# Weights converted by a leaky rectifier, a rounding copy and an integer addition; softmax sums in PSUM, pooled scale in the queries

## The chip, the cores and the metric

One core of a Trainium2 chip runs the whole program. The metric is the device time of one execution in microseconds (us), less is better. The core has five engines that run side by side, each strictly in the order of its own list of instructions: PE (TensorE, the matrix multiplier, whose weight loads are listed as PEld), DVE (VectorE), ACT (ScalarE), POOL (GpSimd) and SP (SyncE, which here only issues DMA transfers). They wait for one another by semaphores. SBUF is the working memory, PSUM the memory that matmuls write; DVE and ACT reach both, POOL reaches SBUF.

## The reference

Attention over 8 batches, 8 heads, 576 positions and 64 values a head, in two parts that are added: one over a band of neighbours (distance below 4), one over sequences pooled by 4. Then a feed-forward layer over all 4608 tokens.

```python
q_d, k_d, v_d = (a.reshape(B, H, Sd, 4, D).mean(axis=3) for a in (q, k, v))
out_up = np.repeat(sm_attn(q_d, k_d, v_d), 4, axis=2)      # softmax(q k^T / 8) v, pooled
scores = np.where(np.abs(i - j) < 4, q @ k.T / 8, -1e9)     # local band
out_local = softmax(scores) @ v
x = (out_up + out_local) as (4608, 512)
h = x @ w_in                                                # 512 -> 2048
g = np.where(h >= 1, h, np.where(h <= -1, 0, (h + 1) ** 2 / 4))
out = g @ w_out                                             # 2048 -> 512
```

The weights arrive as 64-bit floating point numbers, and the kernel's host part passes them on as pairs of 32-bit words; the device makes 32-bit numbers of them.

## The kernel before

*Attention.* The 64 heads are worked in 32 pairs; pair `n` covers two heads of one batch, so four pairs fill one batch of 576 tokens. `attention(n, ...)` is a generator, and each `yield` is a place where other work can be put between. For one pair: DVE pools queries and keys by sums over four (`qd` L150, `kd` L157), ACT puts `qd` into a block-diagonal tile `q_bd` (L153). PE makes the band's scores in windows of 64 (`sl_ps` L166) and the pooled scores (`sp_ps` L176). For the band, DVE adds the mask (L184) and finds the maxima (L191), POOL subtracts them (L192), ACT takes the exponential (L195), DVE sums the rows (L211), adds 1e-9 (L212), inverts (L213) and scales (L214). For the pooled part, DVE finds three maxima (L202) and multiplies them by minus the scale (L203), ACT takes three exponentials of 96x144 straight out of `sp_ps`, each with its row sum as a second output (L205), DVE adds 1e-9 and inverts (L218, L219), ACT scales (L221). PE transposes both (`tl_ps` L233, `tp_ps` L242), ACT copies them out, PE multiplies them with the values (`pl_ps` L261, `pp_ps` L273), ACT and DVE add the two (`xd` L282, `x` L284), and ACT and POOL split the sum into a high and a low part (`xh` L293, `xl` L294). `sp_ps` has a bank of 512 columns of PSUM, of which 432 are used.

*Weights.* `load_weights(f)` fetches block `f` of 16 of both weight matrices (`raw_i`, `raw_o`, 512 KB each). `convert_weights` makes a 32-bit number of each 64-bit one: the upper word, read as a 32-bit float and scaled by ACT (L319), is brought to the right sign and bits by DVE (L320, L321); DVE masks the exponent (L323), scales the lower word with it (L324) and adds it (L327). ACT rounds the sum to the type that PE multiplies (L329) and POOL keeps the rest (L330). Each of the 32 conversions takes one buffer named `m` from a ring of four tiles of 512 columns (`t512`), which the feed-forward's `u`, `osb` and `first` also use.

*Feed-forward.* `mm1(c, f)` multiplies 384 tokens (chunk `c` of 12) with block `f` of `w_in` into `h_ps` (12 matmuls, L408); ACT, DVE and POOL make `gh` and `gl` of it (L419 to L425). `mm2(c, f)` multiplies these with `w_out` into three accumulators `o_ps` (9 matmuls, L446). Chunk 0 needs the first four pairs, chunk 2 the pairs up to the eighth; the first half of all blocks is done for chunks 0 and 2 before the second half is needed.

*Order.* Two lists of steps (`BEFORE_STEPS`, `FIRST_STEPS`) say in which order pieces of attention (`a0` to `a11`), loads (`w`), conversions (`c`), `mm1` (`s`) and `mm2` (`m`) are written for the beginning; then a loop puts one pair between every few feed-forward steps. The framework's scheduler takes this as priority and decides each engine's own order from it, so that a changed set of instructions moves others too. SP issues all transfers from one list: a load into a buffer that is still in use holds those behind it.

Of the kernel before, what the change touches and what calls it, by code (L numbers as in the profile page):

```python
# [99 lines left out]
def attention_then_ffn(ctx: ExitStack, tc, qT, kT, vw, vp, band, w_in, w_out, out):  # L100
    nc = tc.nc
# [37 lines left out]
    def small(n, tag):  # L139
        return apool.tile([P, n], F32, name=tag, tag=tag, bufs=2)  # L140

    def attention(n, pool_1, pool_2):

        b, p = pairs[n]
        q, k = qk[p] if b == 0 else (loaded["q"], loaded["k"])
        M = 2 * QB


        qd = apool.tile([P, SD], F32, name="qd", tag="qd", bufs=1)
        nc.vector.tensor_reduce(qd, q.rearrange("p (s f) -> p s f", f=FACTOR), axis=AX.X, op=ALU.add)  # L150
# [32 lines left out]
        slf = sl.rearrange("p g r c -> p (g r) c")  # L183
# [4 lines left out]
            op=ALU.add,  # L188
# [14 lines left out]
        nc.vector.tensor_scalar_mul(mx[:M], mx[:M], -scale)  # L203
        for i in range(NQB):
            nc.scalar.activation(  # L205
                sp[:M, i], sp_v[:, i], AF.Exp,
                bias=mx[:M, i : i + 1], scale=scale, accum_out=sm[:M, i : i + 1],
            )
# [3 lines left out]
        nc.vector.tensor_scalar_add(ll, ll, 1e-9)  # L212
        nc.vector.reciprocal(ll, ll)  # L213
        nc.vector.tensor_tensor(  # L214
            slf, slf, ll.unsqueeze(2).broadcast_to([P, NB, WIN]), op=ALU.mult
        )
        yield
        nc.vector.tensor_scalar_add(sm[:M], sm[:M], 1e-9)  # L218
# [51 lines left out]
        for kb in range(NKB):  # L270
            for h in range(2):
                hs = slice(h * D, (h + 1) * D)
# [17 lines left out]
            op=ALU.add,  # L290
# [17 lines left out]
    def temp(name):  # L308
        return mpool.tile([P, 512], F32, name=name, tag="t512", bufs=4)

    def convert_weights(name, f):

        t = raw.pop((name, f))
        tf = t.bitcast(F32)
        m = temp("m")
        mi = m.bitcast(I32)


        nc.scalar.activation(m, tf[:, :, 1], AF.Copy, scale=2.0**-112)  # L319
        nc.vector.scalar_tensor_tensor(m, m, -(2.0**32), m, op0=ALU.mult, op1=ALU.max)  # L320
        nc.vector.tensor_scalar(mi, mi, 3, None, op0=ALU.logical_shift_left)  # L321

        nc.vector.tensor_scalar(t[:, :, 1], mi, 0xFF800000 - (1 << 32), None, op0=ALU.bitwise_and)  # L323
        nc.vector.scalar_tensor_tensor(  # L324
            tf[:, :, 0], t.bitcast(U32)[:, :, 0], 2.0**-52, tf[:, :, 1], op0=ALU.mult, op1=ALU.mult
        )
        nc.vector.tensor_tensor(m, m, tf[:, :, 0], op=ALU.add)  # L327
        w = wpool.tile([P, 2, 512], F32R, name=f"w_{name}{f}", tag=f"w{name}{f}")
        nc.scalar.copy(w[:, 0], m)  # L329
        nc.gpsimd.tensor_tensor(w[:, 1], m, w[:, 0], op=ALU.subtract)  # L330
        weights[name, f] = w
# [197 lines left out]
```

## Time and profile before

| | |
|---|---|
| median of 3 runs | 1023.12 us (1021.39 to 1025.07) |
| profiled execution | 1023.42 us |
| its span, first to last instruction | 1021.6 us |
| PE busy | 968.0 us, 95% |
| DVE busy | 444.4 us, 44% |
| ACT busy | 518.7 us, 51% |
| POOL busy | 410.7 us, 40% |

The profile is of one execution. A view by stretches gives each engine's busy time between two moments, a view by groups puts together the instructions of one line, operation and shape: `x17 | 14.2, 834 | 0.3` are 17 instructions, 14.2 us in all, 834 ns each, and 0.3 us for which the engine sat idle before them, with what ended that idle time. A row of waits gives the engine and line that waited, what it waited for, and the us in total, the times, and the longest. The row PEclk gives PE's granted clock in 40 equal slices, in tenths of full speed.

### The profile page before, as it was taken

How to read it: one execution, taken by the hardware profiler on the slowest of the kernel's cores; microseconds unless marked ns; L12 is line 12 of the kernel's file. 1: busy time of each engine (PE TensorE's matmuls, PEld its weight loads, DVE VectorE, ACT ScalarE, POOL GpSimd, SP SyncE). 2: the span in 40 equal slices, each digit the busy share in tenths (PEclk: the TensorE clock that was granted, in tenths of full speed). 3: DMA queues.
4: the chain of work that ended last, by engine and by line, in shares of the span. 5: the costliest groups of instructions: out<-in, count | busy, mean ns of one | idle time of the engine just before them, and what ended most of it. 6: DMA issues, size and time to landing. Idle time of an engine off the chain costs nothing.

```text
span 1021.6 us, 18401 instructions
## 1 busy us (share of the span) xinstructions
PE 968.0 (95%) x7412; PEld 851.1 (83%) x7412; DVE 444.4 (44%) x774; ACT 518.7 (51%) x1189; POOL 410.7 (40%) x359
## 2 busy tenths in 40 slices
PE   5577898999999999999999999999999999999998
PEld 4465687889988888999888888899888888899997
DVE  7999979754344533112433443111443344111111
ACT  5556564545455655434655565433655546433433
POOL 3566655453345444322435444322443544222221
PEclk8579899999999999999999999999999999999999
DMA  7666410000133311100212311100311320000000
GB/s 267 220 232 209 151 56 1 31 24 32 34 117 102 113 48 50 55 1 24 80 48 69 102 54 49 56 1 1 102 49 48 98 72 21 31 1 1 32 1 31
DMA packets 28261, 69.37 MB, mean 68 GB/s; under 512 B 3344, under 2 KB 3344, under 8 KB 28176
## 3 DMA queue, kind: packets, MB, share of 16 engines
q1 hardware_dynamic: 28176, 68.20, 20.7%
q8 instruction: 58, 0.95, 0.4%
q14 instruction: 27, 0.22, 0.1%
HBM read 57.18 MB, written 11.01 MB: 67 GB/s over the span
## 4 chain that ended last, share of the span: by engine, by line
PE 79%; DVE 12%; issue 3%; ACT 3%; POOL 1%; DMA 1%; SPq 0%; DVEq 0%; ACTq 0%; POOLq 0%
PE h_ps L408 35%; PE o_ps L446 34%; PE sp_ps L176 2%; PE sl_ps L166 2%; DVE m L320 2%; PE pl_ps L261 2%; PE pp_ps L273 2%; PE tl_ps L233 2%; PE tp_ps L242 1%; DVE m L327 1%; DVE raw_o L324 1%; DVE raw_i L324 1%; DVE u L421 1%; DVE raw_o L323 1%; DVE m L321 1%
## 5 line engine op out<-in xcount | busy, mean ns | idle before, releaser
L408 PE MATMUL h_ps<-xh,w_i 128*128 128x384 f32 x1536 | 403.4, 344 | 7.5 <-DVE u L421 5.2
L425 POOL TENSOR_TENSOR gl<-u,gh 128x384 fp32r<-128x384 f32 x192 | 208.2, 1085 | 480.3 <-ACT gh L424 374.4
L446 PE MATMUL o_ps<-w_o,gh 128*128 128x512 f32 x1152 | 358.4, 392 | 1.6 <-ACT gh L424 1.6
L408 PEld LDWEIGHTS h_ps<-xh,w_i 128*128 128x128 f32 x1536 | 277.7, 190 | 24.2 <-DVE u L421 7.1
L421 DVE SCALAR_TENSOR_TENSOR u<-h_ps,u 128x384 f32<-128x384 f32 x192 | 106.5, 555 | 435.8 <-ACT u L420 409.5
L408 PE MATMUL h_ps<-xl,w_i 128*128 128x384 f32 x768 | 261.8, 341 | 2.7 <-POOL xl L294 2.7
L446 PEld LDWEIGHTS o_ps<-w_o,gh 128*128 128x128 f32 x1152 | 213.2, 188 | 35.7 <-ACT gh L424 2.5
L446 PE MATMUL o_ps<-w_o,gl 128*128 128x512 f32 x576 | 226.4, 393 | 1.3 <-POOL gl L425 1.3
L419 ACT ACTIVATE u<-h_ps 128x384 f32<-128x384 f32 x192 | 94.1, 491 | 179.6 <-PE h_ps L408 173.4
L424 ACT CAST gh<-u 128x384 fp32r<-128x384 f32 x192 | 98.4, 513 | 103.8 <-DVE u L421 102.5
L408 PEld LDWEIGHTS h_ps<-xl,w_i 128*128 128x128 f32 x768 | 145.9, 190 | 3.8 <-POOL xl L294 3.4
L446 PEld LDWEIGHTS o_ps<-w_o,gl 128*128 128x128 f32 x576 | 108.3, 188 | 25.7 <-POOL gl L425 2.9
L420 ACT ACTIVATE u<-u 128x384 f32<-128x384 f32 x192 | 100.2, 523 | 4.8
L205 ACT ACTIVATE sp<-sp_ps,mxp 96x144 f32<-96x144 f32 x96 | 35.1, 369 | 62.7 <-DVE mxp L203 60.8
L192 POOL TENSOR_TENSOR sl<-sl,mxl 128x640 f32<-128x640 f32 x32 | 41.2, 1288 | 56.2 <-DVE mxp L203 41.7
L225 POOL TENSOR_TENSOR vh<-vp_sb 72x512 f32<-72x512 f32 x32 | 45.5, 1422 | 16.7 <-DMA vp_sb<-vp 5.8
L294 POOL TENSOR_TENSOR xl<-x,xh 128x576 fp32r<-128x576 f32 x32 | 46.9, 1464 | 9.2 <-ACT xh L293 9.1
L284 DVE TENSOR_TENSOR x<-pl_ps,xd 128x576 f32<-128x576 f32 x32 | 24.2, 755 | 47.3 <-ACT xd L282 45.9
L233 PE MATMUL tl_ps<-ident,sl 128*128 128x128 f32 x160 | 25.7, 295 | 16.7 <-DVE sl L214 9.7
L176 PE MATMUL sp_ps<-kd,q_bd 128*96 128x144 f32 x192 | 34.1, 318 | 7.3 <-DVE kd L157 7.1
L233 PEld LDWEIGHTS tl_ps<-ident,sl 128*128 128x128 f32 x160 | 20.2, 150 | 23.3 <-DVE x L284 7.0
L184 DVE TENSOR_TENSOR sl<-sl_ps,band_sb 128x640 f32<-128x640 f32 x32 | 26.2, 820 | 28.5 <-PE sl_ps L166 28.5
(59 smaller groups left out, 847.4 us busy)
## 6 DMA issues: line engine op xcount, KB each, us to landing
v_sb<-vw SPq DMA_DIRECT2D x32, 320.0 KB
vp_sb<-vp SPq DMA_DIRECT2D x32, 288.0 KB
raw_i<-w_in SPq DMA_DIRECT2D x16, 512.0 KB
raw_o<-w_out SPq DMA_DIRECT2D x16, 512.0 KB
q_sb<-qT SPq DMA_DIRECT2D x28, 288.0 KB
k_sb<-kT SPq DMA_DIRECT2D x28, 288.0 KB
out<-osb SPq DMA_DIRECT2D x30, 256.0 KB
partial<-osb SPq DMA_DIRECT2D x6, 256.0 KB
```

Of the source, the lines that this page charges most:

```text
L176: nc.tensor.matmul(sp_v[:, i, :], q_bd[:, i, :], kd, start=True, stop=True)
L192: nc.gpsimd.tensor_tensor(slf, slf, ml.unsqueeze(2).broadcast_to([P, NB, WIN]), op=ALU.subtract)
L225: nc.gpsimd.tensor_tensor(vh, vpt[:, :, 0:2, :], vpt[:, :, 2:4, :], op=ALU.add)
L233: nc.tensor.transpose(tl_v[:, g * P : (g + 1) * P], sl[:, g].rearrange("p r c -> p (r c)"), ident)
L294: nc.gpsimd.tensor_tensor(xl[:, p, r0 : r0 + S], x, xh[:, p, r0 : r0 + S], op=ALU.subtract)
L408: nc.tensor.matmul(h[:, :TCH], wi[:, wt, cc * P : (cc + 1) * P], xt[:, cc, ts], start=(n == 0), stop=(n == 3 * NCC - 1),)
L419: nc.scalar.activation(u, h[:, :TCH], AF.Relu, bias=0.5, scale=0.5)
L420: nc.scalar.activation(u, u, AF.Square)
L421: nc.vector.scalar_tensor_tensor(u, h[:, :TCH], 1.0, u, op0=ALU.max, op1=ALU.min)
L424: nc.scalar.copy(gh, u)
L425: nc.gpsimd.tensor_tensor(gl, u, gh, op=ALU.subtract)
L446: nc.tensor.matmul(o, gt[:, ts], wo[:, wt, :], start=starts and n == 0, stop=ends and n == 2)
```

## The change

Three parts.

*Conversion.* The scaled copy and DVE's first operation become one ACT operation, a leaky rectifier with the slope -2^32 on the negative side. A second ACT operation takes the lower words as unsigned integers, scales them by 2^-29 and rounds them to an integer into a new buffer `low` from the same ring as `m`. DVE shifts `m` by three bits as before and then adds `low` as an integer. The masking, the scaling of the lower word and the floating addition are gone: of five operations on DVE two are left, of one on ACT (beside the rounding at the end) there are two. The integer addition is built as an instruction of its own on 1024 16-bit halves.

*Sums.* The row sums of the band and of the pooled part stand in 13 unused columns of `sp_ps` instead of SBUF tiles. The inverse of the pooled sums still goes to `sm` in SBUF.

*Scale.* The pooled scale is multiplied into the queries where they are put into `q_bd`; the exponentials need no scale, and the reduction that finds the maxima writes them negated, so that one small DVE operation goes.

```diff
-            nc.scalar.copy(
-                q_bd[hs, :, h * QB : (h + 1) * QB], qd[hs].rearrange("p (n s) -> p n s", n=NQB)
+            nc.scalar.mul(
+                q_bd[hs, :, h * QB : (h + 1) * QB],
+                qd[hs].rearrange("p (n s) -> p n s", n=NQB),
+                1.0 / (8.0 * FACTOR * FACTOR),
             )
...
-        nc.vector.tensor_reduce(mx[:M], sp_v, axis=AX.X, op=ALU.max)
-        nc.vector.tensor_scalar_mul(mx[:M], mx[:M], -scale)
+        sums = sp_ps[:, NQB * SD : NQB * SD + NB]
+        psums = sp_ps[:M, NQB * SD + NB : NQB * SD + NB + NQB]
+        nc.vector.tensor_reduce(mx[:M], sp_v, axis=AX.X, op=ALU.max, negate=True)
         for i in range(NQB):
             nc.scalar.activation(
-                sp[:M, i], sp_v[:, i], AF.Exp,
-                bias=mx[:M, i : i + 1], scale=scale, accum_out=sm[:M, i : i + 1],
+                sp[:M, i], sp_v[:, i], AF.Exp, bias=mx[:M, i : i + 1], accum_out=psums[:, i : i + 1]
             )
         yield
-        ll = small(NB, "sml")
-        nc.vector.tensor_reduce(ll, slf, axis=AX.X, op=ALU.add)
-        nc.vector.tensor_scalar_add(ll, ll, 1e-9)
-        nc.vector.reciprocal(ll, ll)
+        nc.vector.tensor_reduce(sums, slf, axis=AX.X, op=ALU.add)
+        nc.vector.tensor_scalar_add(sums, sums, 1e-9)
+        nc.vector.reciprocal(sums, sums)
         nc.vector.tensor_tensor(
-            slf, slf, ll.unsqueeze(2).broadcast_to([P, NB, WIN]), op=ALU.mult
+            slf, slf, sums.unsqueeze(2).broadcast_to([P, NB, WIN]), op=ALU.mult
         )
         yield
-        nc.vector.tensor_scalar_add(sm[:M], sm[:M], 1e-9)
-        nc.vector.reciprocal(sm[:M], sm[:M])
+        nc.vector.tensor_scalar_add(psums, psums, 1e-9)
+        nc.vector.reciprocal(sm[:M], psums)
...
-        nc.scalar.activation(m, tf[:, :, 1], AF.Copy, scale=2.0**-112)
-        nc.vector.scalar_tensor_tensor(m, m, -(2.0**32), m, op0=ALU.mult, op1=ALU.max)
+        nc.scalar.activation(m, t.bitcast(F32)[:, :, 1], AF.Prelu, scale=2.0**-112, alpha=-(2.0**32))
+
+        low = temp("low").bitcast(I32)
+        nc.scalar.activation(low, t.bitcast(U32)[:, :, 0], AF.Copy, scale=2.0**-29)
         nc.vector.tensor_scalar(mi, mi, 3, None, op0=ALU.logical_shift_left)
-
-        nc.vector.tensor_scalar(t[:, :, 1], mi, 0xFF800000 - (1 << 32), None, op0=ALU.bitwise_and)
-        nc.vector.scalar_tensor_tensor(
-            tf[:, :, 0], t.bitcast(U32)[:, :, 0], 2.0**-52, tf[:, :, 1], op0=ALU.mult, op1=ALU.mult
-        )
-        nc.vector.tensor_tensor(m, m, tf[:, :, 0], op=ALU.add)
+        nc.vector.tensor_tensor(mi, mi, low, op=ALU.add)
```

The order of the engines' lists changes with it. On DVE, before, from the mask of the third pair (`L184`) to the scaling of its scores (`L214`); the names `raw_i` and `raw_o` are the words of a block, `m` the buffer of a conversion:

```order
L184 TENSOR_TENSOR sl<-sl_ps,band_sb 128x640
L321 TENSOR_SCALAR m<-m 128x512
L191 TENSOR_REDUCE mxl<-sl 128x10
L323 TENSOR_SCALAR raw_i_162<-m 128x512
L202 TENSOR_REDUCE mxp<-sp_ps 96x3
L324 SCALAR_TENSOR_TENSOR raw_i_162<-raw_i_162 128x512
L203 TENSOR_SCALAR mxp<-mxp 96x3
L321 TENSOR_SCALAR m<-m 128x512
L327 TENSOR_TENSOR m<-m,raw_i_162 128x512
L323 TENSOR_SCALAR raw_o_164<-m 128x512
L211 TENSOR_REDUCE sml<-sl 128x10
```

And now, a pair's rows around its scaling (`L215`) and the next one's mask (`L186`); `ISA` is the integer addition:

```order
L219 TENSOR_SCALAR sp_ps<-sp_ps 96x3
L323 TENSOR_SCALAR m<-m 128x512
L220 RECIPROCAL smp<-sp_ps 96x3
L324 ISA m<-m,low 128x1024
L323 TENSOR_SCALAR m<-m 128x512
L324 ISA m<-m,low 128x1024
L206 TENSOR_REDUCE mxp<-sp_ps 96x3
L285 TENSOR_TENSOR x<-pl_ps,xd 128x576
L212 TENSOR_REDUCE sp_ps<-sl 128x10
```

Between the rows of attention stand two operations of a conversion where there were five, and two conversions pass where one and a half did. On ACT, at the start of the program, before:

```order
L195 ACTIVATE sl<-sl 128x640
L319 ACTIVATE m<-raw_i_156 128x512
L205 ACTIVATE sp,smp<-sp_ps,mxp 96x144 x3
L319 ACTIVATE m<-raw_o_158 128x512
L221 ACTIVATE sp<-sp,smp 96x144 x3
```

And now the same place, the exponentials of the first pair (`L208`) and the first conversions:

```order
L208 ACTIVATE sp,sp_ps<-sp_ps,mxp 96x144
L197 ACTIVATE sl<-sl 128x640
L208 ACTIVATE sp,sp_ps<-sp_ps,mxp 96x144
L319 ACTIVATE m<-raw_i_156 128x512
L208 ACTIVATE sp,sp_ps<-sp_ps,mxp 96x144
L322 ACTIVATE low<-raw_i_156 128x512
L319 ACTIVATE m<-raw_o_158 128x512
L322 ACTIVATE low<-raw_o_158 128x512
L326 CAST w_i_259<-m 128x512
L326 CAST w_o_296<-m 128x512
```

The three exponentials of a pair no longer stand in a row: the second and the third carry a wait for the one before, and other work is put between them. `L212` on DVE carries a wait for the third. Four operations and both roundings of the first two conversions now stand ahead of the first pair's scaling. On SP, before, from the third pair's `v_sb` to the fourth's:

```order
L136 DMA v_sb<-vw 128x640
L305 DMA raw_o_430<-w_out 128x1024
L133 DMA vp_sb<-vp 72x1024
L130 DMA q_sb<-qT 128x576
L130 DMA k_sb<-kT 128x576
L136 DMA v_sb<-vw 128x640
```

And now:

```order
L136 DMA v_sb<-vw 128x640
L133 DMA vp_sb<-vp 72x1024
L306 DMA raw_i_687<-w_in 128x1024
L306 DMA raw_o_689<-w_out 128x1024
L306 DMA raw_i_700<-w_in 128x1024
L306 DMA raw_o_702<-w_out 128x1024
L306 DMA raw_i_842<-w_in 128x1024
L306 DMA raw_o_844<-w_out 128x1024
L136 DMA v_sb<-vw 128x640
```

Six loads of raw weights stand between the two where one stood.

More of the change, by code (lines that the diff above doesn't have):

```diff
@@ L198, in attention @@
         sp = apool.tile([P, NQB, SD], F32, name="sp", tag="sp", bufs=1)
-        scale = 1.0 / (8.0 * FACTOR * FACTOR)
         mx = small(NQB, "mxp")
         sm = small(NQB, "smp")
-        nc.vector.tensor_reduce(mx[:M], sp_v, axis=AX.X, op=ALU.max)
-        nc.vector.tensor_scalar_mul(mx[:M], mx[:M], -scale)
+        sums = sp_ps[:, NQB * SD : NQB * SD + NB]
+        psums = sp_ps[:M, NQB * SD + NB : NQB * SD + NB + NQB]
+        nc.vector.tensor_reduce(mx[:M], sp_v, axis=AX.X, op=ALU.max, negate=True)
         for i in range(NQB):
             nc.scalar.activation(
-                sp[:M, i], sp_v[:, i], AF.Exp,
-                bias=mx[:M, i : i + 1], scale=scale, accum_out=sm[:M, i : i + 1],
+                sp[:M, i], sp_v[:, i], AF.Exp, bias=mx[:M, i : i + 1], accum_out=psums[:, i : i + 1]
             )
         yield
-        ll = small(NB, "sml")
-        nc.vector.tensor_reduce(ll, slf, axis=AX.X, op=ALU.add)
-        nc.vector.tensor_scalar_add(ll, ll, 1e-9)
-        nc.vector.reciprocal(ll, ll)
+        nc.vector.tensor_reduce(sums, slf, axis=AX.X, op=ALU.add)
+        nc.vector.tensor_scalar_add(sums, sums, 1e-9)
+        nc.vector.reciprocal(sums, sums)
         nc.vector.tensor_tensor(
-            slf, slf, ll.unsqueeze(2).broadcast_to([P, NB, WIN]), op=ALU.mult
+            slf, slf, sums.unsqueeze(2).broadcast_to([P, NB, WIN]), op=ALU.mult
         )
         yield
-        nc.vector.tensor_scalar_add(sm[:M], sm[:M], 1e-9)
-        nc.vector.reciprocal(sm[:M], sm[:M])
+        nc.vector.tensor_scalar_add(psums, psums, 1e-9)
+        nc.vector.reciprocal(sm[:M], psums)
         for i in range(NQB):
@@ L313, in convert_weights @@
         t = raw.pop((name, f))
-        tf = t.bitcast(F32)
         m = temp("m")
         mi = m.bitcast(I32)
-        nc.scalar.activation(m, tf[:, :, 1], AF.Copy, scale=2.0**-112)
-        nc.vector.scalar_tensor_tensor(m, m, -(2.0**32), m, op0=ALU.mult, op1=ALU.max)
+        nc.scalar.activation(m, t.bitcast(F32)[:, :, 1], AF.Prelu, scale=2.0**-112, alpha=-(2.0**32))
+        low = temp("low").bitcast(I32)
+        nc.scalar.activation(low, t.bitcast(U32)[:, :, 0], AF.Copy, scale=2.0**-29)
         nc.vector.tensor_scalar(mi, mi, 3, None, op0=ALU.logical_shift_left)
-        nc.vector.tensor_scalar(t[:, :, 1], mi, 0xFF800000 - (1 << 32), None, op0=ALU.bitwise_and)
-        nc.vector.scalar_tensor_tensor(
-            tf[:, :, 0], t.bitcast(U32)[:, :, 0], 2.0**-52, tf[:, :, 1], op0=ALU.mult, op1=ALU.mult
-        )
-        nc.vector.tensor_tensor(m, m, tf[:, :, 0], op=ALU.add)
+        nc.vector.tensor_tensor(mi, mi, low, op=ALU.add)
         w = wpool.tile([P, 2, 512], F32R, name=f"w_{name}{f}", tag=f"w{name}{f}")
```

## The prediction

> **What bounds the kernel now.** I read the page's chain of waits first, then the busy times of each engine by stage, then the groups of instructions inside the stage that has idle time, and last who waited there for whom.
>
> ```profile
> PE 79%; DVE 12%; issue 3%; ACT 3%; POOL 1%; DMA 1%; SPq 0%; DVEq 0%; ACTq 0%; POOLq 0%
> PEclk8579899999999999999999999999999999999999
> 0.00:8.00 8.00, 2.29 (x43) 2.16 (x44) 2.33 (x3) 1.90 (x3) 1.67 (x8) 1.00 0.72 209
> 8.00:135.00 127.00, 90.98 (x1016) 73.28 (x1014) 123.02 (x193) 74.72 (x185) 77.04 (x57) 0.80 0.61 207
> 135.00:250.00 115.00, 108.36 (x536) 95.78 (x537) 79.94 (x116) 59.66 (x124) 52.92 (x43) 0.97 0.06 21
> 250.00:1021.00 771.00, 766.35 (x5821) 679.85 (x5819) 239.17 (x463) 382.47 (x878) 279.03 (x253) 1.00 0.16 50
> ```
>
> The columns of the last four rows are the stretch, its length, and the busy us of PE, PEld, DVE, ACT and POOL, then PE's clock and the DMA's share and GB/s. After 250 us PE is busy 766.35 of 771 us at full clock: nothing that DVE or ACT gives up there can shorten the run. From 8 to 135 us, in which the first eight pairs of heads pass, DVE is busy 123.02 of 127 us (97%), PE 90.98 at a clock of 0.80, ACT 74.72 (59%), POOL 77.04. That stage is bound by DVE, and the chain agrees: its 12% of DVE is about 123 us.
>
> ```profile
> PE tl_ps L233 <- DVE sl L214: 9.7, 3, 6.4
> PE tl_ps L233 <- DVE x L284: 4.8, 2, 3.2
> ACT xh L293 <- DVE x L284: 6.3, 6, 3.8
> ACT w_i L329 <- DVE m L327: 5.0, 3, 3.0
> ACT w_o L329 <- DVE m L327: 4.8, 4, 2.8
> PE h_ps L408 <- DVE u L421: 4.1, 3, 2.4
> ```
>
> The first five are waits in 8 to 135 us, the last in 150 to 200 us. PE waits there for DVE's results and not for weights to land: the longest single one is 6.4 us for the scaling of `sl`.
>
> **The change part by part.** These are the groups of DVE in 8 to 135 us that the change touches, and L184 beside them:
>
> ```profile
> L320 DVE SCALAR_TENSOR_TENSOR m<-m 128x512 f32<-128x512 f32 x17 | 14.2, 834 | 0.3 <-ACT m L319 0.3
> L321 DVE TENSOR_SCALAR m<-m 128x512 int32<-128x512 int32 x17 | 13.1, 773 | 0.0
> L214 DVE TENSOR_TENSOR sl<-sl,sml 128x640 f32<-128x640 f32 x8 | 10.1, 1264 | 0.0
> L324 DVE SCALAR_TENSOR_TENSOR raw_o<-raw_o 128x512 f32<-128x512 uint32 x8 | 8.9, 1114 | 0.0
> L324 DVE SCALAR_TENSOR_TENSOR raw_i<-raw_i 128x512 f32<-128x512 uint32 x8 | 8.2, 1022 | 0.0
> L327 DVE TENSOR_TENSOR m<-m,raw_i 128x512 f32<-128x512 f32 x8 | 6.9, 857 | 0.0
> L327 DVE TENSOR_TENSOR m<-m,raw_o 128x512 f32<-128x512 f32 x8 | 6.3, 783 | 0.0
> L323 DVE TENSOR_SCALAR raw_o<-m 128x512 int32<-128x512 int32 x8 | 6.3, 782 | 0.0
> L323 DVE TENSOR_SCALAR raw_i<-m 128x512 int32<-128x512 int32 x8 | 5.9, 739 | 0.0
> L212 DVE TENSOR_SCALAR sml<-sml 128x10 f32<-128x10 f32 x8 | 5.9, 736 | 0.0
> L218 DVE TENSOR_SCALAR smp<-smp 96x3 f32<-96x3 f32 x8 | 3.2, 401 | 0.0
> L203 DVE TENSOR_SCALAR mxp<-mxp 96x3 f32<-96x3 f32 x8 | 2.4, 303 | 0.0
> L184 DVE TENSOR_TENSOR sl<-sl_ps,band_sb 128x640 f32<-128x640 f32 x7 | 5.6, 806 | 0.0
> ```
>
> *Conversion on DVE.* L320, L321, L323, L324 and L327 take 14.2+13.1+12.2+17.1+13.2 = 69.8 us in the stage, for about 16.5 conversions. Afterwards 17 conversions stand ahead of the eighth pair's `x` on DVE, each a shift (773 ns as now) and an integer addition, which the trace does not show. It treats 512 words as 1024 halves: its floor is an unblocked 512-element addition, its ceiling 1024 elements at the rate of an unblocked L214:
>
> ```profile
> L327 DVE TENSOR_TENSOR m<-m,raw_i x16: 674/689/1776, 18.3 to 216.5; 128x512 f32<-128x512 f32 x16
> L214 DVE TENSOR_TENSOR sl<-sl,sml x32: 811/825/2232, 14.5 to 867.5; 128x640 f32<-128x640 f32 x32
> L212 DVE TENSOR_SCALAR sml<-sml x32: 157/163/1906, 13.7 to 867.1; 128x10 f32<-128x10 f32 x32
> ```
>
> Columns: shortest/median/longest ns. The floor is 0.67 us, the ceiling 1024 x 811/640 = 1.30 us, or 1.78 us where the addition is held up as L327's longest was. I take 0.83, the mean of L327's two groups, which is the same form on the same bytes: 17 x (0.77+0.83) = 27 us, between 24 and 43.
>
> *Sums in PSUM.* L203 goes (2.4 us, the reduction negates instead). L214, L212 and L218 keep their work but read or write `sp_ps`. In the stage they last 1264, 736 and 401 ns, where over the whole run L214's and L212's medians are 825 and 163: in the stage they are held up. No row shows DVE writing PSUM, so the gain lies between nothing and 8 x (1264-811 + 736-157) = 8.3 us, plus about 2 for L218. A loss is unlikely by the group that streams as many elements out of PSUM, L184: 806 ns, as much as L214 unblocked. I take 8.3+2, with L203 12.6 us. The Trainium skill, "SBUF — State Buffer", section "Who interferes with whom", says that a VectorE instruction with two SBUF inputs, or in a two-port mode, contends with GpSimd, one blocking the other for a whole instruction, and that one with at most one SBUF input does not. The spread of L214 and L212 fits that. By the rule these 10 us go for certain, without it perhaps none; the forecast stands either way, since DVE falls below ACT in both.
>
> DVE's load in the stage is then 123.0 - 69.8 - 12.6 + 27 = 68 us (78 without the PSUM gain): no longer the bound.
>
> *ACT.* The same stage's groups there:
>
> ```profile
> L205 ACT ACTIVATE sp<-sp_ps,mxp 96x144 f32<-96x144 f32 x24 | 8.7, 369 | 1.8 <-PE tp_ps L242 1.0 <-DVE mxp L203 0.7
> L319 ACT ACTIVATE m<-raw_i 128x512 f32<-128x512 f32 x9 | 6.0, 670 | 2.9 <-POOL w_i L330 2.8
> L329 ACT CAST w_i<-m 128x512 fp32r<-128x512 f32 x8 | 4.9, 617 | 5.0 <-DVE m L327 5.0
> L205 ACT ACTIVATION_READ_ACCUMULATOR sp<-sp_ps,mxp 96x1 f32 x24 | 4.6, 194 | 0.0
> L195 ACT ACTIVATE sl<-sl 128x640 f32<-128x640 f32 x8 | 5.9, 738 | 5.3 <-POOL sl L192 5.3
> L424 ACT CAST gh<-u 128x384 fp32r<-128x384 f32 x8 | 4.1, 508 | 0.8 <-DVE u L421 0.7
> ```
>
> The rectifier takes the place of L319's scaled copy with the same operands (670 ns; I see no reason for another time, bounds 617 and 738 from L329 and L195). The rounding copy is new, reads with the same stride as L319: 17 x 0.67 = 11.4 us, between 10.5 and 12.5. The scale in the queries is the same instruction count, and counts nothing. The three exponentials of a pair now each wait for the one before, as each writes its sum into the bank it reads; before, the accumulator read overlapped the next one. Bounds nothing and 2 x 0.194 us a pair; I take half, 1.6 us for eight pairs. By the eighth `xh`, half a conversion more (0.7) and one more eviction of `h_ps` (about 1.5) stand ahead. ACT: 74.7+11.4+1.6+0.7+1.5 = 90 us.
>
> *The added wait.* The row sums L212 now wait for the pair's third exponential, where they waited for `sl`'s exponential alone. Behind them on DVE stand a conversion's shift and addition and `kd`, on which PE's `sp_ps` waits. At 369+194 ns each the three take 1.7 us, so at most 14 us of standing DVE in the stage, of which DVE has 127-68 to spare; the cover is gone only if the pair's own chain sets the end.
>
> *How long the stage becomes.* If ACT ran as tightly as DVE does now, 90/0.97 = 93 us, it would end at 101. PE's side is slower:
>
> ```profile
> 8.00:60.00 52.00, 32.16 (x441) 26.63 (x441) 49.80 (x83) 29.64 (x76) 27.48 (x22) 0.61 0.67 233
> 68.00:135.00 67.00, 52.43 (x548) 41.13 (x548) 65.22 (x98) 41.99 (x100) 44.85 (x33) 0.95 0.56 185
> 60.65 1.01 PE L408 MATMUL h_ps<-xh,w_i 128*128 128x384 f32 x2
> 484.61 2.08 PE h_ps L408 x12
> 486.69 2.06 PE o_ps L446 x9
> ```
>
> The first `h_ps` comes at 60.65. Up to there ACT has 29.6 us and gets eight rounding copies and two more conversions (5.4+2.6): 37.6, which at 83% takes 45 us, so about 53. From 60.65 to 135 lie 74 us, in which PE is idle 67-52.43 = 14.6 in the stretch from 68 alone. In the new order 17 `h_ps` and 5 `o_ps` more stand ahead of the eighth pair's last `pp_ps`, by the last two rows 17 x 0.173 + 5 x 0.229 = 4.1 us. Two thirds of the idle time gone: 74+4.1-10 = 68, so the end is 121. Of 101 and 121 I take 116, nearer to PE's, because ACT, DVE and PE alternate and PE comes out of the first 60 us at a clock of 0.61. **The stage ends 19 us earlier, with 4.1 us more of PE's work done. From 135 to 250 us the 4.1 us of waits for `u` shrink: -3** (bounds 0 and -6.6, the stretch's idle time).
>
> Sum: the profiled execution took 1023.4 us (span 1021.6, 1.8 around it; the median of three is 1023.1). 1023.4 - 19 - 4.1 - 3 = **997.3 us**.
>
> **The rivals.**
> *ACT takes DVE's place without slack:* end at 101, 1023.4 - 34 - 4.1 - 5 = 980. For it: DVE manages 97%. Against: PE's clock and its own work.
> *New waits eat half:* the row sums behind the exponentials, and six loads of raw weights (6 x 512 KB = 3.1 MB, at 207 GB/s 15 us) that SP now issues ahead of the fourth pair's `v_sb`, so that its `pl_ps` is late. End at 126: 1023.4 - 9 - 4.1 - 1 = 1009. Against: those loads go out while SP waits for the third pair anyway.
> *DVE stays the bound, because the addition is far slower than an addition.* 123.0 - 69.8 - 12.6 + 17 x 0.77 = 53.7 us without it; (123.0-53.7)/17 = 4.1 us each would fill DVE again: 1023. The ceiling above is 1.8.
> *Slower: ACT stalls in order.* `low` takes a second buffer of the ring of four that `m`, `u` and `osb` share, so ACT's rectifier waits for POOL's subtraction to free one, with the exponentials behind it; ACT already waits 2.8 us that way (L319). It decides at 90/(127+4.1) = 69% of ACT busy. At 65% the stage takes 138 us: 1023.4 + 11 - 4.1 = 1030. Against: ACT idles now mostly for DVE, which gets free. The Trainium skill, "ScalarE: Activation LUTs", section "Rules for kernel authors", says to put relu, max and the like on VectorE and not on ScalarE; by it this rival would be likelier. Here the row speaks the other way: L320 takes 834 ns on DVE, L319 670 on ACT.
>
> **How the numbers follow.** A measurement of this kernel tells about 0.3% (3 us) from no change. Forecast (989 to 1006) 0.53; ACT without slack (under 989) 0.12; half eaten (1006 to 1020) 0.19; DVE still the bound (1020 to 1026) 0.07; slower 0.09. Faster 0.84, same 0.07, slower 0.09. The range 981 to 1014 leaves out the last two cases, a third of the half-eaten one and none of the bounds above but the extreme.
>
> **What would show it.** In 8 to 116 us: DVE near 68 us, ACT near 90 and the busiest of the two; first `h_ps` near 53; the eighth `xh` near 116; the addition under 1.3 us and L214's counterpart near 0.82; no second table load; PE after 250 us as full as before. It would be wrong if ACT idles for POOL's buffers, if `tl_ps` waits for `sl` as long as now, or if the gain comes after 250 us.

## The result

| | before | after |
|---|---|---|
| median | 1023.16 us (1021.39 to 1025.07, 4 runs) | 1005.58 us (1004.22 to 1008.21, 4 runs) |
| ratio | 1 | 0.983, 95% interval 0.980 to 0.986 |
| profiled execution, span | 1021.6 us | 1002.4 us |

The change is faster by 17.6 us (1.7%) where 26 were forecast, inside the range. Its page shows the chain of waits and the clock that PE was granted; the rows by stretches have the columns of the prediction's (length, busy us of PE, PEld, DVE, ACT, POOL, clock, DMA).

```profile
PE 85%; ACT 1%; DVE 1%; POOL 1%; issue 0%; DVEq 0%; ACTq 0%; POOLq 0%
PEclk8699999999999999999999999999999999999999
```

```profile
8.00:121.00 113.00, 89.04 (x1025) 73.90 (x1025) 75.35 (x138) 81.47 (x203) 70.20 (x58) 0.86 0.68 233
121.00:236.00 115.00, 112.21 (x579) 100.66 (x580) 44.60 (x69) 70.84 (x147) 50.39 (x44) 1.00 0.08 29
236.00:1002.00 766.00, 761.78 (x5771) 676.12 (x5769) 242.63 (x438) 380.41 (x868) 267.60 (x250) 1.00 0.16 50
```

DVE's 12% has gone from the chain. The eighth pair's `xl` now starts at 121.0 instead of 134.6 us, and ahead of it DVE is busy 75 of 113 us instead of 123 of 127. In the 115 us behind that moment PE stood still 6.6 us before (115 - 108.36) and stands still 2.8 now, at a clock of 1.00 instead of 0.97. So far the gain comes where it was forecast. Of the 26.1 us of the prediction's sum the profiled pair shows 19.2 (1023.42 against 1004.22), so some 7 are missing there, and 8.5 between the medians. To see where they went, a mark is needed that every run passes after about the same work. I take the casts of `gh`, of which each of the 192 feed-forward steps has one: the 45th lies behind the stage that the change is about. The rows of the cast's line, up to the 45th and in the whole run, of before and of after; the columns are shortest/median/longest ns, then the first and the last start in us:

```profile
L424 ACT CAST gh<-u x45: 497/513/526, 72.4 to 307.6; 128x384 fp32r<-128x384 f32 x45
L424 ACT CAST gh<-u x192: 497/513/526, 72.4 to 1013.7; 128x384 fp32r<-128x384 f32 x192
```

```profile
L421 ACT CAST gh<-u x45: 493/513/525, 64.4 to 282.6; 128x384 fp32r<-128x384 f32 x45
L421 ACT CAST gh<-u x192: 493/513/525, 64.4 to 994.5; 128x384 fp32r<-128x384 f32 x192
```

At the 45th cast the changed kernel is 25.0 us ahead (307.6 - 282.6), about the 26.1 of the prediction's sum. At the last it is 19.2 ahead, the difference of the spans. **The other 147 steps take 711.9 us instead of 706.1**: 5.8 us are lost where neither kernel converts weights and where PE waits 0.9 us in all for other engines before and 0.3 after. That became the question, though not at once.

The mark is not quite the same work in both. PE's matmuls of the band's scores behind the 45th cast, in before and after:

```profile
L166 PE MATMUL sl_ps<-k_sb,q_sb x800: 217/218/267, 328.4 to 861.2; 64*64 64x64 f32 x160
L168 PE MATMUL sl_ps<-k_sb,q_sb x840: 217/218/268, 285.0 to 841.0; 64*64 64x64 f32 x168
```

The changed kernel has the scores of one pair more there (with `sp_ps` and `pp_ps` that is 2.2 us from start to start) and six `o_ps` matmuls fewer (1.4 us). So 0.8 of the 5.8 us is work that moved behind the mark, and 5.0 are a loss.

### The profile page after: what moved, and what is told of

It is laid out like the page before. It is cut to its first block, busy times and chain, and to the rows that moved or that the text cites. A ratio compares the mean times of both kernels' runs of the same rounds, so it can differ in the third digit from the quotient of the medians.

```text
span 1002.4 us, 18310 instructions
## 1 busy us (share of the span) xinstructions
PE 964.6 (96%) x7412; PEld 852.2 (85%) x7412; DVE 364.1 (36%) x646; ACT 534.6 (53%) x1221; POOL 389.5 (39%) x359
## 4 chain that ended last, share of the span: by engine, by line
PE 85%; ACT 1%; DVE 1%; POOL 1%; issue 0%; DVEq 0%; ACTq 0%; POOLq 0%
PE h_ps L405 38%; PE o_ps L443 37%; PE sp_ps L178 2%; PE sl_ps L168 2%; PE pl_ps L262 2%; PE pp_ps L274 2%; PE tp_ps L243 1%; PE tl_ps L234 1%; POOL xl L295 0%; POOL sl L194 0%; POOL gl L422 0%; ACT u L417 0%; ACT u L416 0%; DVE sp_ps L212 0%; ACT gh L421 0%
## 5 line engine op out<-in xcount | busy, mean ns | idle before, releaser
L422 POOL TENSOR_TENSOR gl<-u,gh 128x384 fp32r<-128x384 f32 x192 | 195.4, 1018 | 505.6 <-ACT gh L421 391.0
L208 ACT ACTIVATE sp<-sp_ps,mxp 96x144 f32<-96x144 f32 x96 | 36.1, 376 | 46.4 <-DVE mxp L206 44.0
L226 POOL TENSOR_TENSOR vh<-vp_sb 72x512 f32<-72x512 f32 x32 | 42.0, 1312 | 17.0 <-DMA vp_sb<-vp 6.1
L212 DVE TENSOR_REDUCE sp_ps<-sl 128x10 f32<-128x640 f32 x32 | 26.5, 827 | 33.0 <-ACT sp L208 17.1
L222 ACT ACTIVATE sp<-sp,smp 96x144 f32<-96x144 f32 x96 | 34.8, 405 | 4.4 <-DVE smp L220 4.4
L234 PE MATMUL tl_ps<-ident,sl 128*128 128x128 f32 x160 | 23.9, 282 | 13.5 <-DVE sl L215 13.5
L186 DVE TENSOR_TENSOR sl<-sl_ps,band_sb 128x640 f32<-128x640 f32 x32 | 26.3, 823 | 28.2 <-PE sl_ps L168 28.2
```

Of the source, the lines that this page charges most:

```text
L208: nc.scalar.activation(sp[:M, i], sp_v[:, i], AF.Exp, bias=mx[:M, i : i + 1], accum_out=psums[:, i : i + 1])
L226: nc.gpsimd.tensor_tensor(vh, vpt[:, :, 0:2, :], vpt[:, :, 2:4, :], op=ALU.add)
L422: nc.gpsimd.tensor_tensor(gl, u, gh, op=ALU.subtract)
```

## The experiments

All ratios are to the kernel before on the same chip, with the 95% interval. "First `h_ps`" is the start of PE's first feed-forward matmul; "rest" is the time from the 45th to the last cast; "distance" is the mean from one `h_ps` matmul's start to the next within a step, between 640 and 700 us of the span. These three are worked out from the starts in each trace. After, e2, e9 and e11 have that other pair's scores behind the mark, e3, e4, e5, e7, e8 and e10 four `sp_ps` matmuls more than before (0.4 us); e1, e6 and e12 have the work of before there. The last column says where the weights, and all that is allocated behind them, stand in SBUF: "b" as in the kernel before, "a" as in the changed one, 128 bytes lower.

| run | median us | ratio | first `h_ps` | 45th cast | rest | distance ns | place |
|---|---|---|---|---|---|---|---|
| before | 1023.16 | 1 | 60.65 | 307.6 | 706.1 | 173.4 | b |
| after | 1005.58 | 0.983 (0.980 to 0.986) | 58.23 | 282.6 | 711.9 | 176.5 | a |
| e1 | 999.51 | 0.977 (0.976 to 0.979) | 52.32 | 284.1 | 705.7 | 173.3 | b |
| e2 | 1030.72 | 1.008 (1.006 to 1.009) | 66.20 | 309.1 | 711.8 | 176.5 | a |
| e3 | 1012.42 | 0.989 (0.986 to 0.991) | 51.84 | 293.4 | 711.3 | 176.7 | a |
| e4 | 998.24 | 0.976 (0.974 to 0.978) | 52.86 | 282.1 | 706.4 | 173.4 | b |
| e5 | 999.92 | 0.977 (0.976 to 0.979) | 55.59 | 283.1 | 706.4 | 173.4 | b |
| e6 | 999.68 | 0.977 (0.975 to 0.978) | 58.04 | 285.1 | 705.7 | 173.4 | b |
| e7 | 1024.50 | 1.002 (1.001 to 1.002) | 57.30 | 308.6 | 706.4 | 173.4 | b |
| e8 | 1007.26 | 0.984 (0.983 to 0.986) | 54.34 | 290.7 | 706.4 | 173.4 | b |
| e9 | 1001.67 | 0.977 (0.975 to 0.980) | 59.22 | 285.6 | 707.6 | 173.4 | b |
| e10 | 1004.14 | 0.981 (0.979 to 0.983) | 52.60 | 284.5 | 711.2 | 175.7 | weights at 55296 |
| e11 | 1012.01 | 0.988 (0.986 to 0.991) | 59.06 | 287.2 | 716.8 | 174.9 | weights at 55296 |
| e12 | 1027.66 | 1.005 (1.003 to 1.006) | 60.11 | 307.3 | 710.1 | 176.5 | a |

### First theory: the row sums' wait in the shared bank

What showed first in the changed trace was the first `h_ps`, at 58.2 where 53 was forecast. The timeline of the third pair, from the last of its three exponentials (columns: start, us, engine and line, and in brackets the idle time ahead with what ended it), shows the wait that the change adds:

```profile
48.26 0.39 ACT L208 ACTIVATE sp<-sp_ps,mxp 96x144 f32<-96x144 f32 x1
48.53 0.18 ACT L208 ACTIVATION_READ_ACCUMULATOR sp<-sp_ps,mxp 96x1 f32 x1
48.74 0.83 DVE L212 TENSOR_REDUCE sp_ps<-sl 128x10 f32<-128x640 f32 x1 [2.62 <-ACT sp L208]
...
53.27 0.71 PE L234 MATMUL tl_ps<-ident,sl 128*128 128x128 f32 x5
```

The row sums start only when the third exponential is through, and PE's transpose follows them. In the first round "bank theory" held this wait responsible, and "ACT theory" the rounding copies on ACT.

**e1: the new conversion alone**, the softmax part as before. **e2: the softmax part alone**, the conversion as before.

> The new conversion alone, softmax sums and scale as before. Bank theory (the row sums' wait for the pair's third exponential, which shares their PSUM bank, holds the first 58 us of the changed kernel): without that wait the first h_ps comes at 52 to 55 us, DVE carries about 80 us in 8 to 122 us because the band's scaling and small additions are held up by POOL again, total 999 to 1004 us. ACT theory (the rounding copies on ACT hold it): first h_ps at 57 to 59 us as in the changed kernel, total 1004 to 1008 us.

> Sums in PSUM and scale in the queries alone, conversion as before. DVE stays the bound at about 110 of 123 us in the stage: 1011 to 1016 us if its freed time counts in full; bank theory: the new wait eats part of it, 1014 to 1021 us; if the PSUM operands free nothing, 1021 to 1025 us. The scaling of sl lasts 0.82 us without spread if the move to PSUM ends its hold-ups.

**e3, e4: the changed kernel with the row sums elsewhere**, in the bank of the band's scores, or in SBUF.

```diff
-        sums = sp_ps[:, NQB * SD : NQB * SD + NB]
+        sums = sl_ps[:, 0, 0:NB]        # e3
+        sums = small(NB, "sml")         # e4
```

> As the changed kernel, but the band's row sums stand in unused columns of sl_ps instead of sp_ps, so that they no longer wait for the exponentials. Bank theory: first h_ps at 50 to 54 us, DVE waits nothing for ACT sp in the stage (8.1 us in the changed kernel), total 997 to 1002 us. ACT theory: first h_ps at 57 to 59 us, total 1004 to 1007 us.

> As the changed kernel, but the band's row sums stand in SBUF as before the change; the pooled sums stay in PSUM. Bank theory: the wait is gone as in the kernel with the sums in sl_ps, but the scaling of sl (0.82 us now) is held up by POOL again to above 0.95 us in the stage: first h_ps at 51 to 55 us, total 998 to 1003 us, 0 to 3 us above that kernel. ACT theory: 1004 to 1008 us.

The first `h_ps` came at 52.3, 51.8 and 52.9 in e1, e3 and e4, and e1 and e4 ran in 999.5 and 998.2 us, as the bank theory wanted. But e3, equally free of the wait, took 1012.4, and e2 was 8 us slower than before, worse than either theory had it. Whoever stops after e1 and e4 has a wrong explanation with two confirmations.

**e5: meant as the wait without the bank.** Row sums in SBUF as in e4, and DVE's two small operations on the pooled sums, which need the third exponential, written ahead of them.

```diff
+        nc.vector.tensor_scalar_add(psums, psums, 1e-9)
+        nc.vector.reciprocal(sm[:M], psums)
         nc.vector.tensor_reduce(sums, slf, axis=AX.X, op=ALU.add)
...
-        nc.vector.tensor_scalar_add(psums, psums, 1e-9)
-        nc.vector.reciprocal(sm[:M], psums)
```

> The changed kernel with the row sums in SBUF, and the two VectorE instructions on the pooled sums (+1e-9 and reciprocal) put ahead of the row sums' reduction. The row sums again stand behind the third exponential, now by VectorE's order and not by a bank; nothing else is moved. Wait theory (the row sums' standing behind the third exponential is what costs, wherever the sums lie): first h_ps back at 57 to 60 us, as in the changed kernel (58.2), time 1003 to 1008 us. Placement theory (sums in PSUM cost in another way): first h_ps 52 to 54, time 997 to 1001.

**e6: e4 with the pooled sums in SBUF too** (`psums = sm[:M]`). **e7: e2 with the row sums in SBUF.**

> The changed kernel with the row sums and the pooled sums in SBUF: of the softmax part only the scale in the queries and the negated maximum are left. Both theories on the row sums: 997 to 1001 us, first h_ps 52 to 54, no difference from the kernel with the row sums alone in SBUF (998.2) beyond 1.5 us. If the exponentials' waits on the pooled sums' bank cost what the prediction put in (0.2 us a pair): 1 to 2 us faster than 998.2. If the pooled sums in PSUM are worth their ended hold-ups (L218 401 to 153 ns): 1 to 3 us slower.

> The kernel before with the softmax part of the change, but with the row sums in SBUF. With the row sums in PSUM this was 1030.7 us, 7.7 slower than before. Wait theory: the row sums' wait is all of that loss, so 1018 to 1023 us (before, or a little faster for the dropped L203), first h_ps 59 to 61, and the wait of tl_ps for sl shrinks from 19.0 us in all to about 15 or less. Rival (the loss lies in the pooled sums, the scale or the negated maximum): 1027 to 1031 us.

e5 ran in 999.9 us, with the first `h_ps` at 55.6. That looks like the end of the wait theory, but its trace shows that the edit did not bring the wait. The framework's scheduler decides DVE's order, and in six of the first eight pairs the row sums (L214) begin before the third exponential has ended, as they do in seven of e4's. The fourth pair of e5, with its last two exponentials:

```profile
41.96 0.36 ACT L208 ACTIVATE sp<-sp_ps,mxp 96x144 f32<-96x144 f32 x1
42.31 0.81 DVE L214 TENSOR_REDUCE sml<-sl 128x10 f32<-128x640 f32 x1
42.79 0.38 ACT L208 ACTIVATE sp<-sp_ps,mxp 96x144 f32<-96x144 f32 x1
43.25 0.17 DVE L212 TENSOR_SCALAR sp_ps<-sp_ps 96x3 f32<-96x3 f32 x1
```

So e5 is e4 once more and says nothing of the wait; the run that does is e9, below. e6 has no such wait, and yet its first `h_ps` came at 58.0; it ran in 999.7. So that mark, on which the theory had been built, says nothing of the total. e7 gave back 6.2 us of e2's 1030.7, between what the two theories wanted.

### Where the 6 us lie

The column "rest" sorts the runs cleanly: 705.7 to 706.4 in before, e1, e4 to e8; 711.3 to 711.9 in after, e2 and e3. The last three have their row sums in PSUM. At equal work behind the mark, e3 lies 4.9 us above e4. But the loss also accrues in steps that contain no attention, so no sums at all. Here is one such step of PE in the changed kernel: the first `h_ps` matmul, the first of `o_ps` after twelve of `h_ps`, and the next step's start.

```profile
662.63 0.52 PE L405 MATMUL h_ps<-xh,w_i 128*128 128x384 f32 x2
...
664.75 0.62 PE L443 MATMUL o_ps<-w_o,gh 128*128 128x512 f32 x2
...
666.79 0.52 PE L405 MATMUL h_ps<-xh,w_i 128*128 128x384 f32 x2
```

Twelve `h_ps` take 2.12 us, nine `o_ps` 2.04. In e9, below, the same step:

```profile
663.37 0.52 PE L406 MATMUL h_ps<-xh,w_i 128*128 128x384 f32 x2
...
665.45 0.62 PE L444 MATMUL o_ps<-w_o,gh 128*128 128x512 f32 x2
...
667.51 0.52 PE L406 MATMUL h_ps<-xh,w_i 128*128 128x384 f32 x2
```

There they take 2.08 and 2.06. PE is full in both; its matmuls simply follow each other at another pace, those of `h_ps` faster in e9 and those of `o_ps` a little slower (228.2 ns from start to start between 640 and 700 us, 227.0 in the changed kernel). What after, e2 and e3 share beside the sums in PSUM is that the SBUF tile `sml` is no longer allocated. It has two buffers of 10 words, which occupy 128 bytes of each partition with their rounding up, and everything allocated behind them moves down. The compiled programs have these addresses (bytes in a partition):

| | `xh` | `w_i` of block 0 | ring `t512` | `gh` |
|---|---|---|---|---|
| before, e1, e4 to e9 | 18432 | 113600 | 211904 | 220096 |
| after, e2, e3, e12 | 18432 | 113472 | 211776 | 219968 |
| e10 | 18432 | 88064 | 211904 | 220096 |
| e11 | 18432 | 88064 | 211776 | 219968 |

**e9: the changed kernel, instruction for instruction, with `sml` reserved and not used.**

```diff
+        small(NB, "sml")
         sums = sp_ps[:, NQB * SD : NQB * SD + NB]
```

> The changed kernel, instruction for instruction, with the two unused buffers of sml still reserved, so that all that lies behind them in SBUF (vh to k, the weights, the ring t512, gh, gl) has the addresses of the kernel before: 128 bytes higher than in the changed kernel. Layout theory: in the three kernels without sml the matmuls of h_ps follow each other every 175 to 178 ns, in all others every 173.3, in steps without attention too, which is 34 ns for each of the 148 last steps, about 5 us; so here 173 to 174 ns and 999 to 1001.5 us, with the first h_ps late as in the changed kernel (57 to 60 us). Placement theory (row sums in PSUM cost in themselves): 175 to 178 ns, 1004 to 1007 us.

**e12: the kernel before with `sml` gone**, its row sums in a tile that is dead by then; same instructions, sums in SBUF.

```diff
-        ll = small(NB, "sml")
+        ll = ml
```

> The kernel before, with one line changed: the row sums go into the tile mxl, whose values are used up by then, so that sml is not allocated and all that lies behind it in SBUF starts 128 bytes lower, as in the changed kernel. Sums stay in SBUF, conversion and instructions are those of before. Layout theory: h_ps matmuls 176 to 178 ns apart instead of 173.4, 5 to 6 us lost after the first 44 steps of the feed-forward part, none before them: 1027 to 1030 us. Rival (the 128 bytes only cost together with sums in PSUM or the new conversion): 1021 to 1026 us.

The rows of the `h_ps` matmuls between 600 and 780 us, of after, of e9, of before and of e12 in this order, with shortest/median/longest duration:

```profile
L405 PE MATMUL h_ps<-xh,w_i x303: 333/338/443, 599.7 to 779.9; 128*128 128x384 f32 x152
```

```profile
L406 PE MATMUL h_ps<-xh,w_i x303: 332/336/445, 600.9 to 779.9; 128*128 128x384 f32 x152
```

```profile
L408 PE MATMUL h_ps<-xh,w_i x304: 332/336/448, 600.6 to 779.7; 128*128 128x384 f32 x152
```

```profile
L408 PE MATMUL h_ps<-xh,w_i x296: 332/338/441, 601.7 to 776.0; 128*128 128x384 f32 x148
```

338 goes with the lower addresses and 336 with the higher ones, whatever the kernel. (The profile models the ends of matmuls; between their starts the difference is 3 ns.) e9's rest fell from 711.9 to 707.6, with the same work in it, and its time to 1001.7; e12's rest rose from 706.1 to 710.1, with the 45th cast where it was (307.3 and 307.6), and its time to 1027.7, 4.9 us over before on the same chip (1022.77). **128 bytes of address alone cost this kernel some 5 us.** The executions of one kernel differ with PE's mean granted clock, and at like clocks the tests agree: the changed kernel took 1004.2 us at 0.985, 1006.9 at 0.979 and 1008.2 at 0.975, e9 998.0 at 0.985, 1001.6 at 0.980 and 1002.9 at 0.974, so 5 to 6 less. e2 and e7 fit as well: of the 5.9 us between their profiled executions, 5.4 lie in the rest (some of it the other pair's scores) and 0.5 ahead of it.

e9 is also the run that settles the wait. It has the wait of the row sums for the exponential and PE's wait for the scaled `sl` as the changed kernel has them (8.1 and 13.5 us; e4 0 and 6.6). From 8 to 121 us, e9's two rows, then the changed kernel's row of PE:

```profile
DVE sp_ps L213 <- ACT sp L209: 7.9, 4, 3.0
PE tl_ps L235 <- DVE sl L216: 12.7, 3, 4.6
PE tl_ps L234 <- DVE sl L215: 13.5, 3, 4.6
```

At a clock of 0.985 e9 took 998.0 us, and e4, which has no such wait, 997.5 and 998.2; at 0.980 e9 took 1001.6 and 1001.8, e4 1000.6 at 0.979. So the wait costs about 1 us at most, and the wait theory, which had it cost 6, falls.

**e10, e11: e4 and the changed kernel with the weights ahead of attention in SBUF**, from a multiple of 1024 bytes.

```diff
+    wpool = ctx.enter_context(tc.tile_pool(name="weights", bufs=1))
     apool = ctx.enter_context(tc.tile_pool(name="attn", bufs=1))
-    wpool = ctx.enter_context(tc.tile_pool(name="weights", bufs=1))
```

> The kernel with the row sums in SBUF (998.2 us, weights from byte 80832 of each partition, 448 beyond a multiple of 512), with the pool of the weights made ahead of the pool of attention: weights from byte 55296, a multiple of 1024; xh, xl, the ring t512, gh and gl stay. If the weights' address sets the 173.3 ns between h_ps matmuls, another figure: under 173 (some single ones are at 169 now; 4 ns on 192 x 12 matmuls would be 9 us, so 989 to 996 us) or over. If xh, gh or the ring set it: 173.3 and 996 to 1000 us.

> The changed kernel with the same swap of pools: weights from byte 55296, the ring, gh and gl still 128 bytes lower than before, row sums in PSUM. If the weights' address is what the 128 bytes changed: the same spacing of h_ps matmuls as in the kernel with row sums in SBUF and the weights first, and 1 to 3 us above its time. If it is the ring's, gh's or gl's address: 175 to 178 ns as in the changed kernel, 1003 to 1008 us.

Between 600 and 780 us, first e10, then e11; before's `o_ps` matmuls have 389 there in both groups:

```profile
L443 PE MATMUL o_ps<-w_o,gh x222: 388/394/398, 603.0 to 777.2; 128*128 128x512 f32 x111
L443 PE MATMUL o_ps<-w_o,gl x111: 388/388/397, 603.5 to 777.4; 128*128 128x512 f32 x111
```

```profile
L443 PE MATMUL o_ps<-w_o,gh x222: 393/394/398, 602.7 to 778.1; 128*128 128x512 f32 x111
L443 PE MATMUL o_ps<-w_o,gl x111: 390/394/403, 603.2 to 778.4; 128*128 128x512 f32 x111
```

The hoped-for better place was a worse one: rests of 711.2 and 716.8 us, and now `o_ps` pays as well. The weights' address matters (e10 against e4: only it and attention's tiles moved), and what lies 128 bytes lower in e11 matters beside it. (e11's rest also has the other pair's scores, 0.4 us more than e10's.) So it isn't a question of one tile's alignment but of several operands' places; which relation counts, and why, stays open.

### Which engine should round

**e8: e4 with the rounding copy on DVE.**

```diff
-        nc.scalar.activation(low, t.bitcast(U32)[:, :, 0], AF.Copy, scale=2.0**-29)
+        nc.vector.tensor_scalar(low, t.bitcast(U32)[:, :, 0], 2.0**-29, None, op0=ALU.mult)
```

> The changed kernel with the row sums in SBUF, and the rounding copy on VectorE as a multiplication with an integer result, not on ScalarE. It takes 17 x 0.67 = 11.4 us off ACT in the stage and puts 17 x 0.67 to 0.85 = 11 to 14 us on DVE. If ACT's load bounds the stage: under 996 us, first h_ps under 52. If neither load bounds it, but the order of waits and PE's own work and clock: 997 to 1002. If DVE has no slack of this size, since its hold-ups by POOL come back: over 1003.

The same 113 us of e4, then of e8:

```profile
8.00:121.00 113.00, 83.83 (x990) 68.59 (x989) 89.83 (x137) 81.17 (x203) 74.51 (x59) 0.86 0.68 234
```

```profile
8.00:121.00 113.00, 82.29 (x960) 67.95 (x959) 100.77 (x152) 71.56 (x184) 69.99 (x55) 0.82 0.67 229
```

ACT got rid of 10 us and nothing came of it; DVE at 101 of 113 us is near its old load, and the 45th cast comes 8.6 us later (290.7 against 282.1). DVE has some slack now, not this much.

e4 has the lowest median, 998.2 us, 7.3 under the changed kernel; the intervals of e1, e5, e6 and e9 overlap with its own.

## Why the prediction was right, and what it left out

**The stage was DVE's, and the conversion was its price: right.** e1, the conversion alone, gains 23 us (999.5 against 1022.7). The groups of DVE and ACT in the changed kernel from 8 to 121 us, with the columns of the prediction's:

```profile
L324 DVE CUSTOM_DVE_ANT_0 m<-m,low 128x1024 uint16<-128x1024 uint16 x17 | 13.5, 795 | 3.4 <-ACT low L322 2.8
L323 DVE TENSOR_SCALAR m<-m 128x512 int32<-128x512 int32 x17 | 9.7, 572 | 1.6 <-ACT m L319 1.6
L212 DVE TENSOR_REDUCE sp_ps<-sl 128x10 f32<-128x640 f32 x8 | 6.6, 824 | 9.0 <-ACT sp L208 8.1 <-ACT sl L197 0.8
L215 DVE TENSOR_TENSOR sl<-sl,sp_ps 128x640 f32<-128x640 f32 x8 | 6.5, 815 | 0.1
L213 DVE TENSOR_SCALAR sp_ps<-sp_ps 128x10 f32<-128x10 f32 x8 | 1.3, 168 | 0.1
L219 DVE TENSOR_SCALAR sp_ps<-sp_ps 96x3 f32<-96x3 f32 x8 | 1.3, 156 | 0.0
```

```profile
L322 ACT ACTIVATE low<-raw_i 128x512 int32<-128x512 uint32 x9 | 6.0, 671 | 0.0
L319 ACT ACTIVATE m<-raw_i 128x512 f32<-128x512 f32 x9 | 6.0, 669 | 1.3 <-POOL w_i L327 1.2
L208 ACT ACTIVATE sp<-sp_ps,mxp 96x144 f32<-96x144 f32 x24 | 9.0, 374 | 0.7 <-DVE mxp L206 0.5
L208 ACT ACTIVATION_READ_ACCUMULATOR sp<-sp_ps,mxp 96x1 f32 x24 | 3.9, 162 | 0.0
```

*Durations: right.* The integer addition took 795 ns (830 forecast; bounds 670 and 1780), the shift 572 (773), so 17 conversions 23.2 us instead of 27. The rectifier took 669 and the rounding copy 671 (both 670).

*Sums in PSUM, durations: right.* L215, L213 and L219 fell to 815, 168 and 156 ns as forecast, 8 x (1264-815 + 736-168 + 401-156) = 10.1 us, beside L203. Over the whole run the spread is gone:

```profile
L215 DVE TENSOR_TENSOR sl<-sl,sp_ps x32: 807/820/824, 17.4 to 847.3; 128x640 f32<-128x640 f32 x32
```

Before, it was 811/825/2232. In e4, with the row sums back in SBUF, the hold-ups are back, L215 and L213 on average, and the addition longer as well:

```profile
L324 DVE CUSTOM_DVE_ANT_0 m<-m,low 128x1024 uint16<-128x1024 uint16 x17 | 20.0, 1183 | 2.1 <-ACT low L322 1.2
L215 DVE TENSOR_TENSOR sl<-sl,sml 128x640 f32<-128x640 f32 x8 | 9.9, 1236 | 0.1
L213 DVE TENSOR_SCALAR sml<-sml 128x10 f32<-128x10 f32 x8 | 3.3, 409 | 0.1
```

The rule of the Trainium skill ("SBUF — State Buffer", section "Who interferes with whom") that an instruction of DVE with at most one SBUF input, outside the two-port modes, does not contend with GpSimd agrees with L215's 807 to 824 ns. *What they are worth: nothing.* e4's DVE is busy 90 us in the stage instead of 75, and the 45th cast comes at 282.1 instead of 282.6. With the new conversion these 15 us of DVE have no price. The prediction expected that, but its reason ("DVE falls below ACT in both") does not hold: e4's DVE, with 90 us, is above its ACT with 81. With the old conversion, where DVE was the bound, e2 did not gain at the 45th cast either (309.1 against 307.6): in its first 58 us PE waits 17.7 us for the scaled `sl`, where the kernel before waits 9.7.

```profile
PE tl_ps L234 <- DVE sl L215: 17.7, 3, 7.1
```

*One of the prediction's own signs of being wrong came true.* It was to be wrong "if `tl_ps` waits for `sl` as long as now". That was 9.7 us, and the changed kernel waits 13.5 (its row is shown with e9). The sums in PSUM lengthen this wait in the first 58 us from 9.7 to 17.7 with the old conversion (e2), and with the new one from 5.3 in e1 to 13.5. The sign was a poor one: e9 has the long wait and not the loss.

*DVE's load, 68 forecast, 75 measured: the subtraction was wrong.* 123.0 is time in which DVE did anything; the groups' times overlap at their ends and add up to more (139.4 us for those listed in the stage before). Groups subtracted from such a union take away too much. Among themselves they come out: 139.4 - 69.8 - 12.6 + 23.2 = 80.2, and those listed after add up to 82.2.

*ACT, 90 forecast, 81.5 measured: the same slip the other way.* The durations of ACT's instructions in the stage add up to 97.2 us after and 85.6 before, 11.6 more, as much as the rounding copies alone; the time in which ACT did anything rose by only 6.8 (74.7 to 81.5), since the recorded times of neighbours overlap. The exponentials' waits on each other cost nothing: three with their sums took 3 x (374+162) ns instead of 3 x (369+194).

*The added wait: costed at up to 14 us of standing DVE and hidden. Right.* DVE stood 8.1 us in the stage for it (L212's row), and the changed kernel passes the 45th cast at 282.6 us, e4 without the wait at 282.1. e9 has it too, and took at most about 1 us longer than e4 at like clocks.

*When the gain comes: two terms off, their sum right by luck.* The stage ended 13.6 us earlier, not 19: the end at 116 was taken between 101 and 121, and 121 it was, the end reckoned from PE's side. Up to the eighth `xl` 7 more `h_ps` and 9 more `o_ps` matmuls stand in the trace, by the prediction's 173 and 229 ns 3.3 us (4.1). The stretch behind gave the rest, 25.0 - 13.6 - 3.3 = 8.1 us instead of 3 (0.8 of it the work that moved behind the mark). So 19 was 5.4 too much and 3 was 5.1 too little, and neither error was argued to meet the other. The first `h_ps` at 53 was a poor mark: it lies between 51.8 and 59.2 in the runs with the new conversion, and does not go with their times.

**The step that failed is one that was not worked out at all:** "After 250 us PE is busy 766.35 of 771 us at full clock: nothing that DVE or ACT gives up there can shorten the run." That nothing could shorten it was taken to mean that nothing would change. The term for PE's own pace was left at zero. The tile that the PSUM sums made superfluous moved everything behind it by 128 bytes, the weights among it, and behind the 45th cast that alone costs 4.0 us (e12) to 4.3 (e9). With 0.8 us of moved work it makes up 4.8 to 5.1 of the 5.8; the remaining 0.7 to 1.0 is not accounted for. By these marks 1023.4 - 25.0 + 5.8 = 1004.2, the profiled run.

**The rivals.** "New waits eat half" gives 1009 and so lies nearer to the measured 1005.6 than the forecast of 997.3 does, but both its mechanisms fail: e9 has the wait without the loss, and the changed trace shows no wait of PE for `v_sb`. The addition is not slow, and ACT did not stall for POOL's buffers (1.2 us at L319, 2.8 before). What the trace could have told beforehand was the possibility, not the price: nothing in one profile shows what another address would do.

**Left open:** why e3 is 10.8 us later at the 45th cast than the changed kernel, with nearly the same rest. In its trace PE stands 6.5 us before `pl_ps` for nothing that the profile names (the changed kernel 0.8 in all), and its clock from 121 to 180 us is 0.88 instead of 1.00; what brings this about wasn't tried. e9's 45th cast at 285.6 against 282.6, with the same instructions and waits, goes with PE's granted clock, 0.77 from 8 to 121 us (third figure from the right in its row) against the changed kernel's 0.86; what set the clock is not shown.

```profile
8.00:121.00 113.00, 91.73 (x953) 76.58 (x952) 74.65 (x136) 80.30 (x201) 66.95 (x56) 0.77 0.66 230
```

## What to carry to other kernels

A tile added or dropped moves every tile behind it. Where PE bounds a long stretch, compare its matmuls' spacing there before explaining a difference by waits; keeping the dropped tile reserved is a one-line test. A mark that all runs pass after equal work tells in which stretch a difference arises, once the work behind it has been counted; single landmarks such as a first matmul do not. Where a scheduler decides the engines' order, look in the trace whether an edit brought the order it was made for: e5's did not.

## What the runs showed of the hardware

Successive matmuls of 384 columns with weight loads between, at a granted clock of 1.00 and with PE full, start 173.4 or 176.5 ns apart according to whether the tiles behind `sml`, the weights among them, lie 128 bytes lower in SBUF; those of 512 columns start 228.2 or 227.0 apart with them, and 233 in e11. The Trainium skill ("TensorE: Matmul & The Clock Gate", section "Wait — 56ns, not 53.3ns?") gives back-to-back matmuls a spacing of the columns at 2.4 GHz plus about 2.5 ns, an estimate of 162.5 ns for 384. No run here came down to it, and it has no term for the place. Between the best and the worst placement tried, the 147 steps differ by 11 us (705.7 to 716.8, of which 0.8 is unequal work), about 1% of the run.
